# The first chunk of a fused attention and two-layer MoE kernel: its order from a list of tasks in place of a running budget

## The chip, the cores and the metric

One Trainium2 chip, one core. The metric is the device time of one execution in microseconds (us), the median of the runs shown. A core has five engines, each with its own instruction stream that it works off in order: TensorE (PE; its weight loads are listed apart as PEld), VectorE (DVE), ScalarE (ACT), GpSimd (POOL) and SyncE (SP, which here issues nearly all DMAs). An instruction that reads what another engine writes waits on a semaphore, and all that stands behind it on its engine waits too.

## The reference

```python
kv  = einsum('bhsd,bhse->bhde', k, v)            # 8 batches, 8 heads, 576 tokens, 64 wide
out = einsum('bhsd,bhde->bhse', q, kv)
out = out / sqrt(mean(out**2, -1) + 1e-6) * g_norm
x   = out, heads joined: 4608 tokens x 512
h   = max(max(x @ w1, x @ w2), x @ w3)           # layer 1, 512 -> 768
x   = h @ w_out                                  # layer 2, 768 -> 512
logits = x @ w_gate + log1p(exp(x @ w_noise)) * noise
# each token to its two best of 8 experts:  out += weight * (relu(x @ e_w1) @ e_w2)
```

All operands are float32. A product runs as three passes over values split into a high and a low part: high x high, high x low, low x high.

## The kernel before

The tokens go through in 9 chunks of 512, each as four tiles of 128. A chunk has these stages: attention (`ao`) and its norm (`norm_a` to `norm_c`); the transposes to `xT` (`xtrans_pe`, then the high part by ACT, the low part by DVE); layer 1 as 18 groups g of 12 matmuls (three passes of four, `g1_mm`), where three groups share one output block f of `h` and DVE takes their maximum (`g1_top`, split by `hsplit`); layer 2 (`g2`), 36 matmuls a tile; routing (`route_a`, `route_b`) and the scatter of rows by POOL (`scatter`). Then 25 units of expert work follow, with the weights streamed in.

The first chunk (chunk 0) is also where the layer weights come in. Weight slot s (0 to 8 for layer 1, two groups each; 9 to 11 for layer 2) arrives packed by `load_w1(s)` in one of three staging buffers and is converted in steps over ACT and DVE: `conv_lo` and `conv_sq` (ACT), `conv_hi` (two DVE instructions), `conv_add` (DVE), `conv_top` (DVE, then the high part W by ACT, line 467), `conv_rest` (DVE, the low part, line 473). The first two passes of a group read the high part of W alone, the third reads the low part. For slots 9 to 11, `gate_a` transposes the converted weight on PE and `gate_b` multiplies it by the router weights, so that layer 2 gives the logits as 16 more columns.

To have more for PE to do beside the conversion, half of chunk 1 (256 of its 512 tokens) gets its attention and its layer 1 in chunk 0 as well (`ao_early`, `xt_early`, `g1_early`: 18 groups with 256 columns); chunk 1 then does the other 256.

What sets the order: all instructions are emitted in the order of the Python program. In chunk 0 `layer1_first` decides, with a running account `T` of two times (PE and DVE) that the program adds fixed amounts to. A group is emitted whole, all three passes; `need_w` emits the rest of the slot's conversion ahead of it, and `took` emits conversion steps while the account of DVE is behind that of PE. Accumulators come from two rings of four banks, `hbank` and `abank`, each taken in turn.

Of the kernel before, what the change touches and what calls it, by code (L numbers as in the profile page):

```python
# [31 lines left out]
CST = {}  # L32
# [52 lines left out]
def body(tc, A, dbg=None):  # L85
# [205 lines left out]
    def hTf(f):  # L291
        return hTa[:, f] if f < 4 else hTb[:, f - 4]
# [4 lines left out]
    def g1_mm(g, bank, n, x=xT, t0=0, t1=512):  # L297
        s = slice((g % 2) * 128, (g % 2) * 128 + 128)
        a, b = ((0, 0), (0, 1), (1, 0))[n]
        for k in range(4):  # L300
            PE.matmul(bank[:, 0:t1 - t0], w_in(g)[:, a, k, s], x[b][:, k, t0:t1],  # L301
                      start=n == 0 and k == 0, stop=n == 2 and k == 3)

    def hsplit(f, hm, t0=0, t1=512):
        h = hTf(f)[:, :, t0:t1]
        ACT.activation(h[:, 0], hm, AF.Copy)  # L306
        DVE.tensor_tensor(h[:, 1], hm, h[:, 0].bitcast(F), op=OP.subtract)

    def g1_top(g, bank, hm):
        if g % 3 == 0:  # L310
# [13 lines left out]

    def early(f):
        return XN[f // 2][:, (f % 2) * 256:(f % 2) * 256 + 256]

    def g1_early(g):
        need_w(g // 2)
        bank = hbank()  # L330
        for z in range(3):
            g1_mm(g, bank, z, xA, 0, 256)
        took(1.42, (0.0, 0.38, 0.38)[g % 3])
        g1_top(g, bank[:, 0:256], early(g // 3))

    rows = RA.rearrange("p (i w) -> p i w", i=4)
    x2b = {}
# [125 lines left out]
    def conv_top(s):  # L463
        sq, f = w_raw(s)
        DVE.scalar_tensor_tensor(wsrc(s), sq, 2.0 ** -30, f, op0=OP.is_ge, op1=OP.mult)
        hi, lo, t = wdst(s)
        ACT.activation(hi, t, AF.Copy)  # L467
        if s + 3 < 12:
            load_w1(s + 3)

    def conv_rest(s):
        hi, lo, t = wdst(s)
# [37 lines left out]
    SP.dma_start(pad[0:64, 0:512], A["kvr"][1][:, 512:1024])  # L510
    kvraw[1] = [quarters(KV0), quarters(STG[2]), (HM[0], pad[:, 0:512])]
    load_w1(1)
    for p in range(4):
# [19 lines left out]
    for i in range(4):  # L533
        ao(0, i, abank())
        norm_a(0, i)
    conv_lo(0)
    norm_b1(0, 0, 4)
    conv_hi(0)
    conv_sq(0)
    norm_b2(0, 0, 4)  # L540
    SP.dma_start(wgn, A["wgn"])
    kvbank, tr = HB[3], []
    for i in range(4):
        norm_c(0, i)
        tr.append(xtrans_pe(0, i, None if i < 3 else abank()))
        xtrans_hi(i, tr[i])
        kv_pair(1, i, kvbank)
    hbank()
    load_q(1)
    load_w1(2)  # L550
    SP.dma_start(pad[:, 0:128], A["cst"][:, CST["tri"][0]:])
    conv_add(0)
    conv_top(0)
    conv_lo(1)
    conv_hi(1)
    conv_sq(1)
    kv_out(1, kvbank)
    for i in range(4):
        xtrans_lo(i, tr[i])
    conv_rest(0)  # L560
    conv_add(1)

    T = {"pe": 26.5, "dve": 31.0}
    steps = []
    for k in range(1, 12):
        if k < 11:
            steps.append((1.92, lambda s: (conv_lo(s), conv_hi(s), conv_sq(s)), k + 1, 0))
        steps.append((1.21, conv_top, k, 1))  # L570
# [3 lines left out]
    ready = {0: 0.0}
    whole = {0}
    gates = {"a": 0, "b": 0}
    ring = [abank]

    def step1():
        cost, fn, k, done = steps.pop(0)  # L580
        if done and k == 11 and gates["a"] == 0:
            do_gate("a")
        fn(k)
        T["dve"] += cost
        if done:
            ready[k] = T["dve"] + 1.1
        if fn is conv_rest:
            whole.add(k)

    def do_gate(x):  # L590
        (gate_a if x == "a" else gate_b)(gates[x], ring[0])
        gates[x] += 1
        T["pe"] += 0.9

    def took(pe, dve):
        T["pe"] += pe
        while steps and T["dve"] + steps[0][0] <= T["pe"]:
            step1()
        if dve:
            T["dve"] = max(T["dve"], T["pe"]) + dve  # L600

    def need_w(k):
        while k not in whole:
            step1()

    def gates_upto(j):
        while gates["b"] <= j:
            need_w(9 + gates["b"])
            if gates["a"] == gates["b"]:
                do_gate("a")  # L610
            do_gate("b")

    def g1_first(g):
        hm = X2f if g // 3 == 4 else HM[0]
        need_w(g // 2)
        if g == 0:
            first = abank(), abank()
            for z in range(3):
                for x in range(2):
                    g1_mm(x, first[x], z)  # L620
            g1_first.banks = list(first)
        bank = g1_first.banks.pop(0) if g < 2 else hbank()
        if g > 1:
            for z in range(3):
                g1_mm(g, bank, z)
        took(2.72, (0.0, 0.69, 0.69)[g % 3])
        g1_top(g, bank, hm)
        if g % 3 == 2 and g < 12:
            hsplit(g // 3, hm)
            T["dve"] += 0.79  # L630

    def ao_early():
        for i in range(2):
            ao(1, i, abank())
            norm_a(1, i, (XN[2], X2f)[i])
        norm_b1(1, 0, 2)
        norm_b2(1, 0, 2)
        for i in range(2):
            norm_c(1, i)
        took(1.9, 3.5)  # L640

    def xt_early():
        for i in range(2):
            t = xtrans_pe(1, i)
            xtrans_hi(i, t, xA)
            xtrans_lo(i, t, xA)
        took(0.9, 1.4)
        ready["x"] = T["dve"]

    def layer1_first():  # L650
        g = e = 0
        inf = 1e9
        while g < 18 or e < 18:
            rg = ready.get(g // 2, inf) if g < 18 else inf
            re = max(ready.get(e // 2, inf), ready.get("x", inf)) if e < 18 else inf
            now = T["pe"]
            if gates["a"] < 3 and ready.get(9 + gates["a"], inf) <= now and gates["a"] == gates["b"]:
                do_gate("a")
                continue
            if rg <= now or (rg < inf and rg <= re and not steps):  # L660
                T["pe"] = max(now, rg)
                g1_first(g)
                g += 1
                if g == 2:
                    ao_early()
                if g == 4:
                    xt_early()
            elif re <= now or (re < inf and not steps):
                T["pe"] = max(now, re)
                g1_early(e)  # L670
                e += 1
            else:
                nxt = min(rg, re)
                if nxt < inf and (not steps or T["dve"] >= nxt):
                    T["pe"] = nxt
                else:
                    step1()
            if gates["b"] < gates["a"]:
                do_gate("b")
        for f in (4, 5):  # L680
            hsplit(f, X2f if f == 4 else HM[0])


    order, spare = unit_order()
# [93 lines left out]
    def misc1(c, g):  # L778
# [14 lines left out]
        if c > 0:  # L793
            if g == 1:
                route_a(c - 1)
            if g == 4:
# [25 lines left out]
    def window(c):  # L822
        nx = c + 1 < NCH

        def fill(i):
            if nx and i < 2:
                ao(c + 1, i + 2, hbank())
                norm(c + 1, i + 2)

        def trans(i):  # L830
            xtrans(c + 1, i) if nx else utrans(0, i)

        if c == 0:
            ring[0] = hbank
            for j in range(3):
                gates_upto(j)
                for i in range(2):
                    g2(0, i, 2 * j, 2 * j + 2)
                if j == 1:
                    while steps:  # L840
                        step1()
                if j > 0:
                    ao(1, j + 1, hbank())
                    norm(1, j + 1, RB[:, j * 512 - 512:j * 512])
# [370 lines left out]
```

## Time and profile before

| what | value |
|---|---|
| median of 3 runs | 1627.76 us (1627.45 to 1629.03) |
| the profiled execution, its own time | 1627.63 us |
| its span in the trace | 1625.9 us |
| mean granted TensorE clock | 0.988 |
| PE busy | 1577.4 us (97%) |
| DVE busy | 743.5 us (46%) |
| ACT busy | 608.4 us (37%) |
| PE busy tenths, the first five of 40 slices | 6, 7, 9, 8, 9 (from the fifth on 9, the last 7) |

The spans of the trace begin with the first instruction. Chunk 0's layer 1 begins at 30.36 us, chunk 1's at 170.23, chunk 2's at 228.26. A row of a timeline gives the start, the duration, the engine, the line and operation, output<-input, and in brackets the engine's idle time ahead of it and who ended that. Equal instructions that follow one another are one row with a count.

### The profile page before, as it was taken

Reading aid. Unit: us, or ns where it says so; the run is one execution under the profiler, and the core shown is the slowest. Engines: PE = TensorE matmul, PEld = TensorE weight load, DVE = VectorE, ACT = ScalarE, POOL = GpSimd, SP = SyncE. Lnnn points to the kernel's source line nnn. Section 1 sums busy time; section 2 is a strip of 40 time slices with the busy share of each in tenths; the row PEclk is TensorE's granted clock in tenths of the full one; section 3 lists DMA queues with packets and bytes.
Section 4 is the critical chain, followed back from the end, with each engine's and each line's share of the span. In section 5 each row is a group of like instructions: output and inputs, shape, how many; then the busy total and the mean of one; then the engine's idle time right before and its main releaser. Section 6 shows DMA issues by size and latency. Waiting matters only on the chain.

```text
span 1625.9 us, 21935 instructions
## 1 busy us (share of the span) xinstructions
PE 1577.4 (97%) x8716; PEld 1370.7 (84%) x8716; DVE 743.5 (46%) x1416; ACT 608.4 (37%) x981; POOL 225.9 (14%) x326
## 2 busy tenths in 40 slices
PE   6798999999999999999999999999999999999997
PEld 6678998988889898989788888888888888888886
DVE  5675443434333343454544355364354444534443
ACT  3443331313232222323233355454354443544433
POOL 0000201111020202021311121111021010210102
PEclk9898999999999999999999999999999999999998
DMA  7220481202030301051554476575474564746543
GB/s 280 97 89 23 175 313 52 105 33 112 26 137 15 123 27 53 1 182 56 197 170 138 125 222 181 182 209 166 156 220 132 179 169 143 206 135 204 146 146 73
DMA packets 52572, 219.43 MB, mean 135 GB/s; under 512 B 6896, under 2 KB 7152, under 8 KB 34928
## 3 DMA queue, kind: packets, MB, share of 16 engines
q1 hardware_dynamic: 32608, 166.50, 28.6%
q0 software_dynamic: 19856, 51.48, 13.6%
q8 instruction: 70, 1.15, 0.3%
q14 instruction: 38, 0.31, 0.1%
HBM read 166.49 MB, written 51.47 MB: 134 GB/s over the span
## 4 chain that ended last, share of the span: by engine, by line
PE 93%; DVE 3%; ACT 1%; DMA 0%; issue 0%; POOL 0%; SPq 0%; DVEq 0%; POOLq 0%; ACTq 0%
PE bank L301 26%; PE bank L1086 24%; PE bank L1024 24%; PE bank L348 10%; PE bank L743 2%; PE bank L188 2%; PE bank L209 2%; PE bank L1038 1%; PE bank L263 1%; DMA G<-mw 0%; PE bank L488 0%; DVE G L452 0%; DVE W L473 0%; DVE G L895 0%; PE bank L212 0%
## 5 line engine op out<-in xcount | busy, mean ns | idle before, releaser
L301 PE MATMUL bank<-B,W 128*128 128x512 f32 (+1 forms) x2160 | 459.9, 373 | 16.9 <-ACT W L467 11.4
L301 PEld LDWEIGHTS bank<-B,W 128*128 128x128 f32 x2160 | 377.6, 191 | 87.2 <-ACT W L467 12.6
L1086 PE MATMUL bank<-W,B 128*128 128x512 f32 x1728 | 421.1, 390 | 0.9 <-ACT hm L1091 0.9
L1086 PEld LDWEIGHTS bank<-W,B 128*128 128x128 f32 x1728 | 320.0, 188 | 64.8 <-ACT hm L1091 1.4
L1024 PE MATMUL bank<-B,W 128*128 128x512 f32 (+1 forms) x1728 | 356.9, 344 | 0.4 <-issue 0.4
L1024 PEld LDWEIGHTS bank<-B,W 128*128 128x128 f32 x1728 | 278.0, 189 | 40.7 <-issue 0.6
L283 DVE TENSOR_TENSOR W<-G,W 128x1024 fp32r<-128x1024 f32 x200 | 242.6, 1225 | 131.6 <-ACT W L282 131.3
L1028 ACT ACTIVATE B<-bank 128x512 fp32r<-128x512 f32 (+1 forms) x176 | 91.5, 520 | 372.0 <-PE bank L1024 354.9
L1029 DVE SCALAR_TENSOR_TENSOR B<-bank,B 128x512 fp32r<-128x512 f32 (+1 forms) x176 | 104.4, 594 | 270.8 <-ACT B L1028 269.0
L282 ACT ACTIVATE W<-G 128x1024 fp32r<-128x1024 f32 x200 | 207.8, 1055 | 47.3 <-PE bank L1086 39.3
L348 PE MATMUL bank<-W,B 128*128 128x256 f32 (+1 forms) x1296 | 172.3, 291 | 0.1
L348 PEld LDWEIGHTS bank<-W,B 128*128 128x128 f32 x1296 | 164.1, 192 | 1.6 <-ACT W L492 0.7
L414 POOL DMA_INDIRECT Xg<-RA,si x72 | 74.5, 1035 | 539.6 <-ACT hm L311 372.2
L313 DVE TENSOR_TENSOR hm<-hm,bank 128x512 f32<-128x512 f32 (+1 forms) x106 | 69.5, 656 | 132.1 <-PE bank L301 128.7
L306 ACT ACTIVATE B<-hm 128x512 fp32r<-128x512 f32 (+1 forms) x53 | 32.2, 607 | 195.2 <-DVE hm L313 174.8
L1024 PE MATMUL bank<-xlo,W 128*128 128x512 f32 x384 | 102.8, 389 | 0.0
L1060 POOL DMA_INDIRECT out<-xn,idt x37 | 62.1, 1677 | 280.9 <-ACT xn L1091 273.7
L1024 PEld LDWEIGHTS bank<-xlo,W 128*128 128x128 f32 x384 | 72.1, 188 | 15.3
L1060 POOL DMA_INDIRECT out<-x2T,idt x19 | 30.9, 1629 | 272.8 <-ACT x2T L1091 270.4
L747 ACT ACTIVATE B<-bank 128x512 fp32r<-128x512 f32 x76 | 41.7, 596 | 45.0 <-PE bank L743 42.3
L311 ACT ACTIVATE hm<-bank 128x512 f32<-128x512 f32 (+1 forms) x53 | 30.5, 576 | 65.9 <-PE bank L301 54.7
L353 ACT ACTIVATE RA<-bank 128x256 f32<-128x256 f32 x72 | 26.1, 386 | 76.0 <-PE bank L348 76.0
(191 smaller groups left out, 1046.1 us busy)
## 6 DMA issues: line engine op xcount, KB each, us to landing
G<-mw SPq DMA_DIRECT2D x100, 1024.0 KB, 4.9
RB<-Xg SPq DMA_DIRECT2D x13, 1028.0 KB, 7.2
G<-w1s SPq DMA_DIRECT2D x12, 1024.0 KB, 5.0
out<-pad POOLq DMA_DIRECT2D x1, 9472.0 KB
kv<-kv SPq DMA_DIRECT2D x8, 1024.0 KB
G<-kv SPq DMA_DIRECT2D x8, 1024.0 KB, 17.1
RB<-qT SPq DMA_DIRECT2D x8, 1024.0 KB, 5.5
RA<-Xg SPq DMA_DIRECT2D x8, 514.0 KB
```

Of the source, the lines that this page charges most:

```text
L282: ACT.activation(w[:, 0:1024], src, AF.Copy)
L283: DVE.tensor_tensor(w[:, 1024:2048], src, w[:, 0:1024].bitcast(F), op=OP.subtract)
L301: PE.matmul(bank[:, 0:t1 - t0], w_in(g)[:, a, k, s], x[b][:, k, t0:t1], start=n == 0 and k == 0, stop=n == 2 and k == 3)
L313: DVE.tensor_tensor(hm, hm, bank, op=OP.max)
L348: PE.matmul(x2b[i][z][:, 0:hi - lo], h[:, a, s], w[:, b, lo:hi], start=f == 0 and n == 0, stop=f == 5 and n == 2)
L414: i = POOL.indirect_dma_start(out=Xg, out_offset=bass.IndirectOffsetOnAxis(ap=idx, axis=0), in_=src, in_offset=None)
L747: ACT.activation(x[0][:, :, s], t, AF.Copy)
L1024: PE.matmul(bank[:, 0:n], w[:, a, k, s], x[b][:, k, 0:n], start=z == 0, stop=z == 11)
L1028: ACT.activation(h[:, 0, 0:n], bank[:, 0:n], AF.Relu)
L1029: DVE.scalar_tensor_tensor(h[:, 1, 0:n], bank[:, 0:n], 0.0, h[:, 0, 0:n].bitcast(F), op0=OP.max, op1=OP.subtract)
L1060: d = POOL.indirect_dma_start(out=A["out"], out_offset=bass.IndirectOffsetOnAxis(ap=idt[u % 3][:, i:i + 1], axis=0), in_=y, in_offset=None ...
L1086: PE.matmul(obank[i], h[:, a, s], w[:, b, ff % 2, :], start=ff == 0 and n == 0, stop=ff == 7 and n == 2)
```

## The change

`layer1_first` with its account `T`, and the code ahead of it from the first conversion on, give way to a list of tasks. Each has a name, an engine, a length, the names of the tasks that it needs, and an urgency; `run_tasks` takes, step after step, the task that can begin first by these lengths (ties within 0.04 go to the lower urgency number) and emits it. Several functions are cut in two for it (`norm_a`, `hsplit`, `conv_top`), and a group of layer 1 becomes two tasks: passes 0 and 1 (`gp`), which need the high part of W, and pass 2 (`gq`), which needs the low part. The matrix work and the conversions are the same instructions in another order. All gates are now emitted ahead of layer 2; `out` emits layer 2 for tiles 0 and 1 behind them. In chunk 1, `route_b` and the first scatter go from group 4 to group 7, the second scatter from group 8 to group 12. `load_w1(s + 3)` still follows the step that frees its buffer.

```diff
-    T = {"pe": 26.5, "dve": 31.0}
...
-    def took(pe, dve):
-        T["pe"] += pe
-        while steps and T["dve"] + steps[0][0] <= T["pe"]:
-            step1()
...
+    def run_tasks(free):
+        end = {}
+        while tasks:
+            best = None
+            for x in tasks:
+                name, eng, cost, after, fn, urgency, hb = x
+                need = list(after)
+                if hb:
+                    taken = ring_users + [hb] * hb[1]
+                    need += [u[0] for u in taken[:-4]]
+                if any(n not in end for n in need):
+                    continue
+                at = max([free[eng]] + [end[n][0] + 0.1 * (end[n][1] != eng) for n in need])
+                key = (at, urgency)
+                if best is None or at < best[0][0] - 0.04 or (at < best[0][0] + 0.04 and urgency < best[0][1]):
+                    best = (key, x)
...
+            fn()
+            end[name] = at + cost + (2.0 if eng == "SP" else 0.0), eng
+            free[eng] = at + cost
...
+        u = 2 + 0.1 * s
+        task(f"lo{s}", "ACT", 1.15, [f"w{s}"], lambda s=s: conv_lo(s), u)
+        task(f"op{s}", "DVE", 1.92, [f"w{s}"] + free_t, lambda s=s: conv_hi(s), u)
...
+        task(f"rest{s}", "DVE", 1.22, [f"hi{s}"], lambda s=s: conv_rest(s), u - 1)
...
+            task(f"gp{g}", "PE", 1.82, ["x0l3", f"hi{g // 2}", "first2"] + ([f"gq{g - 1}"] if g > 2 else []),
+                 lambda g=g: passes(g, [0, 1]), 2, on_ring(f"ev{g}"))
+            task(f"gq{g}", "PE", 0.91, [f"gp{g}", f"rest{g // 2}"], lambda g=g: passes(g, [2]), 1)
...
+    for e in range(18):
+        task(f"eq{e}", "PE", 1.44, ["x1l0", "x1l1", f"rest{e // 2}"] + ([f"eq{e - 1}"] if e else []),
+             lambda e=e: early_passes(e), 3, on_ring(f"ee{e}"))
...
-            if g == 4:
+            if g == (7 if c == 1 else 4):
                 route_b(c - 1)
                 scatter(c - 1, 0)
-            if g == 8:
+            if g == (12 if c == 1 else 8):
                 scatter(c - 1, 1)
...
-            layer1_first()
+            run_tasks({"PE": 16.1, "DVE": 17.4, "ACT": 16.8, "SP": 14.0})
```

Three places of the built order follow. In the names, `W_70` to `W_78` are slots 0 to 8, `G_82` to `G_84` the staging buffers, `B_85` the transposed tokens of chunk 0 and `B_87` those of half of chunk 1, `bank_105` to `bank_108` the ring of `hbank`. The lines of the changed file stand a few lines lower (301 is 308 there, 467 is 474).

ACT around the high part of slot 0 (`W_70`), before:

```order
L267 ACTIVATE B_85<-bank_109,gn 128x4x128
L467 ACTIVATE W_70<-RA 128x1024
L439 ACTIVATE G_83<-G_83 128x1024
L448 ACTIVATE G_83<-G_83 128x1024
L198 COPY kvbd_91<-bank_108 64x4x64
L311 ACTIVATE hm_96<-bank_110 128x512
```

and now:

```order
L274 ACTIVATE B_85<-bank_109,gn 128x4x128
L444 ACTIVATE G_83<-G_83 128x1024
L198 COPY kvbd_91<-bank_108 64x4x64
L474 ACTIVATE W_70<-RA 128x1024
L453 ACTIVATE G_83<-G_83 128x1024
L229 ACTIVATE xn_95<-bank_112 128x512
```

The copy of the second batch's products (`kvbd_91`) and one step of slot 1 now stand ahead of slot 0's high part.

PE in slots 1 to 3 of layer 1, before (12 matmuls are a whole group):

```order
L301 MATMUL bank_105<-B_85,W_71 128x512 x12
L301 MATMUL bank_106<-B_85,W_71 128x512 x12
L263 MATMUL bank_107<-cst,xn_95 128x128 x4
L263 MATMUL bank_108<-cst,x2T_97 128x128 x4
L301 MATMUL bank_105<-B_87,W_70 128x256 x12
L301 MATMUL bank_106<-B_87,W_70 128x256 x12
L301 MATMUL bank_107<-B_85,W_72 128x512 x12
L301 MATMUL bank_108<-B_85,W_72 128x512 x12
```

and now:

```order
L308 MATMUL bank_105<-B_85,W_71 128x512 x12
L308 MATMUL bank_106<-B_85,W_71 128x512 x8
L270 MATMUL bank_107<-cst,xn_95 128x128 x4
L270 MATMUL bank_108<-cst,x2T_97 128x128 x4
L308 MATMUL bank_106<-B_85,W_71 128x512 x4
L308 MATMUL bank_105<-B_87,W_70 128x256 x12
L308 MATMUL bank_106<-B_87,W_70 128x256 x12
L308 MATMUL bank_107<-B_85,W_72 128x512 x8
L308 MATMUL bank_108<-B_87,W_71 128x256 x12
L308 MATMUL bank_107<-B_85,W_72 128x512 x4
L308 MATMUL bank_105<-B_85,W_72 128x512 x12
L308 MATMUL bank_106<-B_85,W_73 128x512 x8
```

From slot 2 on, a group of 256 columns stands between the passes on the high part (x8) and the pass on the low part (x4).

PE at the first gate, before (`wgn` are the router weights, `W_79` is slot 9, in layer 2):

```order
L301 MATMUL bank_108<-B_87,W_78 128x256 x12
L480 MATMUL bank_105<-cst,RA 128x128 x4
L480 MATMUL bank_106<-cst,RA 128x128 x4
L488 MATMUL bank_107<-wgn,G_82 128x16 x8
L348 MATMUL bank_110<-W_79,B_86 128x256
```

and now:

```order
L308 MATMUL bank_108<-B_85,W_78 128x512 x12
L485 MATMUL bank_105<-cst,RA 128x128 x4
L485 MATMUL bank_106<-cst,RA 128x128 x4
L308 MATMUL bank_107<-B_87,W_75 128x256 x12
L308 MATMUL bank_108<-B_87,W_75 128x256 x12
L493 MATMUL bank_105<-wgn,G_82 128x16 x8
L308 MATMUL bank_106<-B_87,W_76 128x256 x12
L485 MATMUL bank_107<-cst,RA 128x128 x4
L485 MATMUL bank_108<-cst,RA 128x128 x4
```

Eight groups of 256 columns are kept back for the three gates and stand between their steps.

## Rows read from the trace of the kernel before

**Rows 1.** Waits of weight loads, 30.3 to 229 us: total, how often, longest

```profile
PEld bank L301 <- ACT W L467: 12.6, 6, 8.5
PEld bank L301 <- DVE W L473: 4.7, 5, 1.4
PEld bank L488 <- ACT G L481: 3.2, 3, 1.9
PEld bank L480 <- DVE RA L465: 3.1, 1, 3.1
PEld L400 <- issue: 2.0, 1, 2.0
PEld bank L301 <- DVE B L272: 1.3, 2, 0.9
PEld bank L301 <- DVE hm L313: 1.2, 1, 1.2
PEld bank L301 <- ACT B L267: 1.2, 1, 1.2
```

**Rows 2.** Stretches: busy us by engine (instructions), then PEclk, DMA share, GB/s

```profile
43.20:53.40 10.20, 6.08 (x14) 4.84 (x15) 5.84 (x6) 2.19 (x2) 0.00 (x0) 0.50 0.31 104
53.50:135.30 81.80, 71.93 (x415) 61.29 (x414) 58.87 (x71) 35.73 (x45) 0.00 (x0) 1.00 0.25 91
135.40:142.20 6.80, 6.80 (x31) 6.62 (x31) 4.05 (x6) 3.09 (x4) 0.00 (x0) 0.50 0.00 0
155.80:159.20 3.40, 3.40 (x18) 3.40 (x17) 0.17 (x1) 0.77 (x2) 1.28 (x5) 0.51 0.03 5
179.70:183.10 3.40, 3.40 (x18) 3.40 (x17) 2.33 (x10) 1.72 (x5) 0.00 (x0) 0.50 0.02 8
```

**Rows 3.** Timeline where layer 1 of chunk 0 begins

```profile
29.37 0.39 PE L188 MATMUL bank<-pad,hm 128*128 128x128 f32 x2
29.86 0.42 DVE L198 COPY kvbd<-bank 64x256 f32<-64x256 f32 x1 [3.04 <-PE bank L188]
30.36 2.11 PE L301 MATMUL bank<-B,W 128*128 128x512 f32 x8 [0.60 <-ACT W L467]
...
37.88 1.16 PE L209 MATMUL bank<-kvbd,kv 128*128 128x128 f32 x8
38.00 0.60 ACT L225 ACTIVATE xn<-bank 128x512 f32<-128x512 f32 x1 [1.34 <-PE bank L212]
```

**Rows 4.** Timeline of PE in chunks 1 and 2, groups back to back

```profile
193.86 6.00 PE L301 MATMUL bank<-B,W 128*128 128x256 f32 x48
...
228.26 11.06 PE L301 MATMUL bank<-B,W 128*128 128x512 f32 x48
```

**Rows 5.** Timeline of DVE, back to back, and of ACT beside it

```profile
72.31 1.06 ACT L467 ACTIVATE W<-RA 128x1024 fp32r<-128x1024 f32 x1 [0.51 <-DVE RA L465]
73.33 0.41 DVE L313 TENSOR_TENSOR xn<-xn,bank 128x256 f32<-128x256 f32 x1
...
73.66 1.22 DVE L473 TENSOR_TENSOR W<-RA,W 128x1024 fp32r<-128x1024 f32 x1
74.80 0.69 DVE L443 TENSOR_SCALAR RB<-G 128x1024 int32<-128x1024 int32 x1
75.52 1.23 DVE L444 SCALAR_TENSOR_TENSOR RB<-G,RB 128x1024 int32<-128x1024 int32 x1
...
76.66 1.22 DVE L465 SCALAR_TENSOR_TENSOR RA<-G 128x1024 f32<-128x1024 f32 x1
```

**Rows 6.** Waits of DVE, 30 to 160 us: total, how often, longest

```profile
DVE hm L313 <- PE bank L301: 11.7, 9, 4.3
```

**Rows 7.** The page's DMA issues: size, median us to landing

```profile
G<-w1s SPq DMA_DIRECT2D x12, 1024.0 KB, 5.0
```

**Rows 8.** Timeline of chunk 1: its first groups, and where DVE comes back

```profile
170.23 5.92 PE L301 MATMUL bank<-B,W 128*128 128x256 f32 x48
...
178.79 0.41 DVE L313 TENSOR_TENSOR hm<-hm,bank 128x256 f32<-128x256 f32 x1
```

More of the change, by code (lines that the diff above doesn't have):

```diff
@@ L574, in body @@
[L574 to L593, printed above, removed]
@@ L595, in took @@
-    def took(pe, dve):
-        T["pe"] += pe
-        while steps and T["dve"] + steps[0][0] <= T["pe"]:
-            step1()
[L599 to L622, printed above, removed]
-        if g > 1:
[L624 to L630, printed above, removed]
@@ L632, in ao_early @@
-    def ao_early():
-        for i in range(2):
[L634 to L665, printed above, removed]
-                if g == 4:
[L667 to L681, printed above, removed]
@@ new lines, in passes, with hm0 @@
+    def passes(g, z):
+        if g not in bank_of:
+            bank_of[g] = abank() if g < 2 else hbank()
+        for n in z:
+            g1_mm(g, bank_of[g], n)
+    def hm0(g):
+        return X2f if g // 3 == 4 else HM[0]
+    for z in range(3):
+        task(f"first{z}", "PE", 1.82, [["x0h3", "hi0", "n0c2"], ["x0l3", "first0"], ["rest0", "first1"]][z],
+             lambda z=z: (passes(0, [z]), passes(1, [z])), 2)
+    for g in range(18):
+        if g > 1:
+            task(f"gp{g}", "PE", 1.82, ["x0l3", f"hi{g // 2}", "first2"] + ([f"gq{g - 1}"] if g > 2 else []),
+                 lambda g=g: passes(g, [0, 1]), 2, on_ring(f"ev{g}"))
+            task(f"gq{g}", "PE", 0.91, [f"gp{g}", f"rest{g // 2}"], lambda g=g: passes(g, [2]), 1)
+        f = g // 3
+        hm_free = [f"split{f - 1}"] if g % 3 == 0 and 0 < f < 4 else ["x1t1"] if g == 12 else []
+        hm_free = ["split3"] if g == 15 else hm_free
+        task(f"ev{g}", "DVE" if g % 3 else "ACT", 0.69 if g % 3 else 0.58,
+             [f"gq{g}" if g > 1 else "first2", "kvp3"] + ([f"ev{g - 1}"] if g else []) + hm_free,
+             lambda g=g: g1_top(g, bank_of[g], hm0(g)), 0.5)
@@ new lines, in body @@
+    last = [f"eq{e}" for e in range(18)]
+    for f in range(6):
+        task(f"hi_h{f}", "ACT", 0.61, [f"ev{3 * f + 2}"] + (last if f > 3 else []), lambda f=f: hsplit_hi(f, hm0(3 * f)), 0.5)
+        task(f"split{f}", "DVE", 0.72, [f"hi_h{f}"], lambda f=f: hsplit_lo(f, hm0(3 * f)), 0.5)
+    x1 = {0: XN[2], 1: X2f}
+    for i in range(2):
+        task(f"ao{i}", "PE", 0.92, ["q1", "kvo", "x0l3"] + (["ao0"] if i else []), lambda i=i: ao(1, i, abank()), 0)
+        task(f"n1s{i}", "ACT", 0.6, [f"ao{i}", f"t0{i + 2}"], lambda i=i: norm_sq(1, i, x1[i]), 0.5)
+        task(f"n1r{i}", "DVE", 0.69, [f"n1s{i}"], lambda i=i: norm_red(1, i), 0.5)
@@ new lines, in early_passes @@
+    def early_passes(e):
+        bank_of["e", e] = hbank()
+        for z in range(3):
+            g1_mm(e, bank_of["e", e], z, xA, 0, 256)
+    for e in range(18):
+        task(f"eq{e}", "PE", 1.44, ["x1l0", "x1l1", f"rest{e // 2}"] + ([f"eq{e - 1}"] if e else []),
+             lambda e=e: early_passes(e), 3, on_ring(f"ee{e}"))
+        task(f"ee{e}", "DVE" if e % 3 else "ACT", 0.42 if e % 3 else 0.36,
+             [f"eq{e}", "x1t0", "x0h3"] + ([f"ee{e - 1}"] if e % 3 else []),
+             lambda e=e: g1_top(e, bank_of["e", e][:, 0:256], early(e // 3)), 0.5)
@@ new lines, in body @@
+    for j in range(3):
+        task(f"gate_a{j}", "PE", 0.9, [f"top{9 + j}"] + ([f"gate_b{j - 1}"] if j else []),
+             lambda j=j: gate_a(j, hbank), 1.5, on_ring(f"gate_a{j}", 2))
+        task(f"gate_w{j}", "ACT", 1.2, [f"gate_a{j}"], lambda: None, 0)
+        task(f"gate_b{j}", "PE", 0.9, [f"gate_w{j}", f"rest{9 + j}"], lambda j=j: gate_b(j, hbank), 1.5,
+             on_ring(f"gate_b{j}"))
+        for i in range(2):
+            task(f"out{i}{j}", "PE", 1.5,
+                 [f"gate_b{j}", f"split{2 * j + 1}", "gq17"] + (["rest11", "gate_a2"] if j == 2 else [])
+                 + ([f"out{i}{j - 1}"] if j else []),
+                 lambda i=i, j=j: g2(0, i, 2 * j, 2 * j + 2), 4 + 0.1 * j + 0.01 * i)
@@ L684, in body @@
+    for i in (2, 3):
+        task(f"ao{i}", "PE", 0.92, ["rest11", f"ao{i - 1}"], lambda i=i: (ao(1, i, hbank()), norm(1, i, RB[:, i * 512 - 1024:i * 512 - 512])),
+             3.5, on_ring(f"ao{i}"))
     order, spare = unit_order()
```

127 lines of the change are left out of this document (70 added, 57 removed).

## The prediction

> **What bounds the kernel now.** I read the page first: PE is busy nearly everywhere except in the first slices, so only the first chunks can give anything large; behind them each chunk is a solid run of matmuls, and a change that ends chunk 1 earlier ends the kernel earlier by as much. Next came the waits of the weight loads from layer 1 of chunk 0 to the start of chunk 2 [rows 1]. I take the weight loads since a matmul's modelled end covers part of a wait, while a late weight load shows all of it. The reader should see two kinds there. Nearly all of it is PE waiting for the weight conversion: for the high part (12.6 us, 8.5 of it at slot 1), for the low part (4.7) and for the gates (3.2 and 3.1). In chunk 1 there are two for the routing, on line 400 (2.0) and on a maximum behind it (1.2). The rows add up to 29.3; 0.6 to 0.8 of that lies ahead of 30.36, where layer 1 begins, so 28.5 are left.
>
> Third, the granted clock [rows 2]. Four stretches ran at half the full clock (0.50, that is 1.2 GHz), and each came behind PE idling or doing little. PE was busy in them for 6.08, 6.80, 3.40 and 3.40 us; what is done at half the clock takes twice as long, so half of 19.68, or 9.8 us, was lost. Waits and clock together: 38.3 us between 30.36 and 228.26 that are no work. This is the ceiling of a better order.
>
> **What is moved, part by part.** The instructions are the same in number and kind; nothing is added or removed but semaphore waits. So the sum is what goes of the 38.3, less what is late in the new order.
>
> *The start.* ACT's high part of slot 0 now stands behind the copy of the second batch's products, which needs PE's last product (29.37 + 0.39 = 29.76). DVE copies its half (to 30.28), ACT its half (I take DVE's 0.42; to 30.75), then the high part takes 1.06 [rows 3, 5]; with three handovers of about 0.1 the first matmul is at 32.1 instead of 30.36: 1.8 us lost. Its bounds are 1.5 (no handovers) and 2.5.
>
> *Slot 1, which waited 8.5 us.* Before, its conversion stood behind the first maximum and the whole norm of chunk 1. Now DVE's order from 30.3 is: first step of slot 1 (0.72 + 1.14), low part of slot 0, add, top (1.14 each), which ends at 35.6. These spacings are between starts in [rows 5]: 0.33 for a 256-wide maximum, 1.14 for a 1024-wide operation of 1.22, 0.72 for line 443, so that a 512-wide operation of about 0.69 costs about 0.61. Then DVE waits for the square of the first attention tile: PE does two passes over two groups (16 matmuls of 11.06 / 48 = 0.230, 3.7 us [rows 4]) and the tile (about 1.1 [rows 3]), until 36.9, ACT squares (0.60 [rows 3]), 37.6. Two reductions, slot 2's first step, a maximum, small ones and the low part of slot 1 come to 5.1: 42.7. PE, which now does both high passes first, gets to that low part at 32.1 + 3.7 + 2 x 1.1 + 16 x 0.230 = 41.7 without counting anything else. So 8.5 becomes 1.0 to 1.6; I take 1.6.
>
> *Slots 2 to 8.* The other 4.1 us for high parts and most of the 4.7 for low parts came in pieces, at slot after slot (the longest for a low part 1.4). In the new order a 256-wide group (12 x 6.00 / 48 = 1.5 us [rows 4]) stands between the high passes and the low pass, which covers the 1.2 of the low part's subtraction. This holds while DVE is ahead. Counted in DVE's new order from the copy at 30.3 to slot 9's top, which releases the first gate: nine slots of 0.72 + 4 x 1.14 (47.5), ten 512-wide maxima, four splits, two reductions, two norms, two low parts of tokens (20 x 0.61 = 12.2), six 256-wide maxima (2.0), small ones (1.0): 62.7, so 93.0, or 95.0 with the 2.0 of waiting above. PE until that gate has 216 wide matmuls (49.7), ten 256-wide groups (15.0) and tiles and transposes (about 3): 32.1 + 67.7 + 2.1 of waits = 101.9. PE is the later one by 7 us; if its 36 operations of 1.14 took their full 1.22, by 4. Both run nearly full, which is new: the lead is small, and I charge 0.5 for late tokens at the first 256-wide group. Weight loads cost nothing: one lands 5.0 us after its issue [rows 7], and it is issued two slots (10.6 us of DVE) ahead of its use; without that cover each slot would lose up to 5.
>
> *The gates.* 6.3 us before. Each now has two 256-wide groups between its transposes and its product, and one ahead of the next gate. The next gate's top stands in DVE behind the previous gate's small evictions, so PE may catch up. Bounds per gate are 0 and 3.1, the longest before; I take 0.8, near the low end, since 4.5 us of PE work stand between: 1.8 for the two that follow a gate and some rest.
>
> *Chunk 1.* The wait on line 400 goes, because that matmul stands three groups later. What is late next is the ring of banks: the sixth group needs the bank of the second, whose maximum stands in DVE behind the routing. It ended 8.97 us after the chunk's start (178.79 + 0.41 - 170.23 [rows 8]), and PE gets there after five groups (7.5 us): 1.5 to 1.9 stays, of 3.2. The moved scatters cost nothing on POOL or in DMA: the last one is four groups (6 us) later, and the rows it reads are overwritten only after the six groups left and the first tile of layer 2; without that cover the copy of the first tile would wait.
>
> *The clock.* Two waits of about 2 us in a row at the start, the gates and the wait in chunk 1 are the places where it can still fall. Of four stretches I keep two short ones like the third and fourth of [rows 2]: 1.7 each, 3.4. Bounds are 0 and the 9.8 of before.
>
> **Sum.** Now lost: 1.8 + 1.6 + 0.5 + 1.8 + 1.9 + 3.4 = 11.0. Gain: 38.3 - 11.0 = 27.3. Against the profiled execution's own 1627.63 (its span and 1.7 around it; the median 1627.76 is 0.1 above) that gives 1600.3; I say 1600.
>
> The Trainium skill, "TensorE: Matmul & The Clock Gate", section "Back-to-back issue gap", gives 131 ns as the sustained spacing of 512-wide matmuls; the trace has 230 [rows 4]. By the page PE's 216 wide matmuls would take 28 instead of 50 us, DVE would be the later one at the first gate (95 against 80), and the sum would be 1593. The measurement decides here, so I give this no chance of its own.
>
> **The rivals.**
>
> *DVE becomes the bound.* Its evictions stand between conversions in a fixed order, and each waits if PE is not there yet. Before, nine of them waited 11.7 us, 1.3 each [rows 6]. If all 16 up to slot 9's top did, DVE would get there at 93.0 + 20.8 = 113.8, 12 after PE: 1612. Against it: PE now has groups of both kinds in stock, so that evictions are mostly due; it decides from 7 us of such waits on.
>
> *The clock stays as patchy as before.* If 9.8 instead of 3.4 are lost: 1607. For it speak the two early waits and the gates; against it that 53.50 to 135.30 ran at 1.00 [rows 2] with the waits of slots 2 to 8 in it.
>
> *The lengths of the list don't hold and nothing is gained.* The order was made for lengths that don't all fit this trace (a start with PE free at 16.1, though it finishes its tiles about then). If slots go on paying their pieces and only the 8.5 shrinks: 28.5 keeps 21, the time is about 1620. The order above speaks against it, since the covering group is there whatever the lengths.
>
> *Slower.* Finer mixing of 512-wide and 256-wide groups with short waits could hold the clock at half over the whole of layer 1 in chunk 0, from 32 to 123. About 85 us of full-clock work would then take up to 85 more. It is slower than before from 31 us of full-clock work run at half (27.3 gained and the 3.4 counted). Half of the stretch would give 1639. Rows of the second stretch [rows 2] speak against it, with a full clock at the same kind of mix.
>
> **How the numbers follow.** Forecast (1594 to 1605) 0.72; DVE bound 0.12; patchy clock 0.09; nothing much gained 0.04; slower 0.03. The low end, 1594, is the sum without any half clock (1597) and with half of the remaining waits gone as well. For eight times in ten I leave out the tail beyond 1608 (most of the DVE case above it, and the two last cases) and what falls below 1594: 1594 to 1608. A change under 0.2% (3.3 us) can't be told from none here. Faster by more: all but the last case and a part of the one before, 0.96; the same: 0.01; slower: 0.03.
>
> **What would show it.** In the changed profile: the first 512-wide group on slot 0 near 32; no wait over 2 us on line 474's high part, and few on the low part between 50 and 100; PE over 95% and DVE over 85% busy there; the first transposes of a gate near 102; chunk 1 near 143 and chunk 2 near 201, after which everything is as before, only earlier. It is wrong in its main step if PE waits for the low or high part at slot after slot, in the clock's term if stretches at 0.50 add up to more than 10 us, and in the claim that the gain is kept if chunk 2 begins early and the span is not shorter by as much.

## The result and the profile after

| | before | after |
|---|---|---|
| median (lowest to highest) | 1627.80 us of 4 runs (1627.45 to 1629.03) | 1599.48 us of 4 runs (1597.54 to 1599.92) |
| profiled execution, its own time | 1627.63 us | 1599.92 us |
| its span | 1625.9 us | 1598.1 us |
| layer 1 of chunk 0 begins | 30.36 us | 31.99 us |
| chunk 1 begins (timeline of the matmuls) | 170.23 us | 143.54 us |
| chunk 2 begins | 228.26 us | 198.90 us |

The ratio is 0.9822 (95% interval 0.9805 to 0.9839): 28.3 us between the medians and 27.7 between the profiled executions, where 27.3 were worked out and 1600 predicted. The page shows where, in its busy times and in PE's busy tenths over 40 slices: of the first four slices, which read 6, 7, 9 and 8 before, the second and the fourth are now 9.

```profile
PE 1567.1 (98%) x8716; PEld 1364.4 (85%) x8716; DVE 742.3 (46%) x1416; ACT 608.4 (38%) x981; POOL 224.7 (14%) x326
PE   6999999999999999999999999999999999999997
```

The waits of the weight loads from layer 1 of chunk 0 to chunk 2 (total, how often, longest) answer to [rows 1]:

```profile
PEld bank L308 <- ACT W L474: 2.2, 1, 2.2
PEld bank L308 <- DVE hm L326: 1.9, 1, 1.9
PEld bank L308 <- DVE W L478: 1.5, 1, 1.5
PEld bank L485 <- DVE RA L470: 1.3, 2, 0.7
PEld bank L308 <- ACT B L274: 0.4, 1, 0.4
PEld bank L212 <- issue: 0.4, 1, 0.4
PEld bank L308 <- DVE B L279: 0.3, 1, 0.3
PEld bank L209 <- issue: 0.2, 1, 0.2
```

The wait for the high part was 12.6 us in six pieces; one is left, at the start. The low part went from 4.7 in five to 1.5 in one, the gates from 6.3 to 1.3, chunk 1 from 3.2 to 1.9. Stretches of the same trace (busy us by engine, then granted clock, DMA share, GB/s) answer to [rows 2]:

```profile
32.72:36.13 3.41, 3.41 (x10) 2.65 (x9) 3.11 (x3) 0.82 (x1) 0.00 (x0) 0.50 1.01 428
50.00:100.00 50.00, 49.89 (x274) 43.57 (x275) 47.48 (x55) 28.47 (x33) 0.00 (x0) 1.00 0.42 148
752.93:756.34 3.41, 3.41 (x13) 2.95 (x13) 3.17 (x10) 1.79 (x3) 0.00 (x0) 0.50 0.00 0
200.00:700.00 500.00, 500.00 (x2883) 439.03 (x2883) 195.93 (x572) 135.87 (x273) 62.59 (x112) 1.00 0.22 82
```

From 50 to 100 us PE is 99.8% busy and DVE 95%, all at the full clock. The only half-clock stretch between layer 1's start and chunk 2 is the first row. The third row is new: it lies far behind, in the expert part. The timeline gives the places that the prediction worked out one by one (start, duration, engine, and in brackets the idle time ahead and who ended it); it answers to [rows 3] and [rows 8] (the last row before a jump can stop where the stretch that was asked for stops, and its count with it):

```profile
30.05 0.42 DVE L198 COPY kvbd<-bank 64x256 f32<-64x256 f32 x1 [0.81 <-PE bank L188]
...
30.50 0.37 ACT L198 COPY kvbd<-bank 64x256 f32<-64x256 f32 x1 [2.13 <-DVE kvbd L198]
30.88 1.06 ACT L474 ACTIVATE W<-RA 128x1024 fp32r<-128x1024 f32 x1
31.99 1.19 PEld L308 LDWEIGHTS bank<-B,W 128*128 128x128 f32 x5 [2.23 <-ACT W L474]
...
38.59 0.60 ACT L229 ACTIVATE xn<-bank 128x512 f32<-128x512 f32 x1 [5.06 <-PE bank L212]
...
43.12 1.22 DVE L478 TENSOR_TENSOR W<-RA,W 128x1024 fp32r<-128x1024 f32 x1
44.39 0.77 PEld L308 LDWEIGHTS bank<-B,W 128*128 128x128 f32 x4 [1.51 <-DVE W L478]
...
98.42 1.22 DVE L470 SCALAR_TENSOR_TENSOR RA<-G 128x1024 f32<-128x1024 f32 x1
102.16 1.02 PEld L485 LDWEIGHTS bank<-cst,RA 128*128 128x128 f32 x8
...
152.56 2.94 PEld L308 LDWEIGHTS bank<-B,W 128*128 128x128 f32 x24 [1.86 <-DVE hm L326]
```

The chain at the start is there as described: DVE's copy, ACT's copy, the high part of slot 0, and then PE. The first gate's transposes begin at 102.16 (102 was expected), 2.5 us after the slot's top ended at 99.64. The waits of DVE from 30 to 160 us show that its evictions into `hm` are now nearly always due, against 11.7 us in [rows 6]. With those into `xn` and `x2T`, which [rows 6] does not list, 20.7 us became 3.0. What it waits for at the start is the square of the first attention tile:

```profile
DVE stat L233 <- ACT xn L229: 3.3, 1, 3.3
DVE hm L326 <- PE bank L308: 1.7, 5, 0.6
```

### The profile page after: what moved, and what is told of

The parts are those of the page before. It is cut to its first block, busy times and chain, and to the rows that moved or that the text cites. A ratio compares the mean times of both kernels' runs of the same rounds, so it can differ in the third digit from the quotient of the medians.

```text
span 1598.1 us, 21920 instructions
## 1 busy us (share of the span) xinstructions
PE 1567.1 (98%) x8716; PEld 1364.4 (85%) x8716; DVE 742.3 (46%) x1416; ACT 608.4 (38%) x981; POOL 224.7 (14%) x326
## 4 chain that ended last, share of the span: by engine, by line
PE 96%; DVE 1%; DMA 1%; ACT 1%; issue 0%; POOL 0%; SPq 0%; POOLq 0%; DVEq 0%
PE bank L308 27%; PE bank L1092 25%; PE bank L1030 25%; PE bank L353 10%; PE bank L760 2%; PE bank L188 2%; PE bank L209 2%; PE bank L1044 1%; PE bank L270 1%; DMA RB<-qT 1%; DMA G<-mw 0%; PE bank L493 0%; PE bank L212 0%; POOL out L1066 0%; PE bank L485 0%
## 5 line engine op out<-in xcount | busy, mean ns | idle before, releaser
L353 PE MATMUL bank<-W,B 128*128 128x256 f32 (+1 forms) x1296 | 167.5, 287 | 0.0
L1066 POOL DMA_INDIRECT out<-hm,idt x19 | 33.0, 1736 | 143.6 <-ACT hm L1097 139.9
```

The source lines that it names most:

```text
L353: PE.matmul(x2b[i][z][:, 0:hi - lo], h[:, a, s], w[:, b, lo:hi], start=f == 0 and n == 0, stop=f == 5 and n == 2)
L1066: d = POOL.indirect_dma_start(out=A["out"], out_offset=bass.IndirectOffsetOnAxis(ap=idt[u % 3][:, i:i + 1], axis=0), in_=y, in_offset=None ...
```

## The experiments

All ratios are to the kernel before, run beside each; `gates_last`, `dve_load`, `dve_load2` and `start` ran on another chip than the other experiments. Chunk 2 is where its first 512-wide group starts in the profiled run. The last column is the span from there on.

| run | median us (runs) | ratio, 95% interval | chunk 2 | behind it |
|---|---|---|---|---|
| before | 1627.80 (4) | 1 | 228.26 | 1397.6 |
| after | 1599.48 (4) | 0.9822 (0.9805 to 0.9839) | 198.90 | 1399.2 |
| slot1_first | 1626.86 (8) | 0.9994 (0.9983 to 1.0006) | 229.18 | 1397.1 |
| route_only | 1626.14 (10) | 0.9993 (0.9984 to 1.0003) | 225.33 | 1399.1 |
| lengths_one | 1612.55 (2) | 0.9901 (0.9872 to 0.9930) | 212.96 | 1399.1 |
| whole_groups | 1599.29 (2) | 0.9820 (0.9791 to 0.9848) | 199.01 | 1398.7 |
| gates_last | 1598.04 (2) | 0.9814 (0.9784 to 0.9844) | 199.89 | 1397.2 |
| route_back | 1602.05 (2) | 0.9837 (0.9808 to 0.9865) | 202.28 | 1397.3 |
| dve_load | 1598.18 (2) | 0.9815 (0.9786 to 0.9843) | 198.69 | 1397.2 |
| dve_load2 | 1602.05 (2) | 0.9839 (0.9810 to 0.9867) | 202.21 | 1398.6 |
| start | 1594.83 (2) | 0.9794 (0.9766 to 0.9823) | 195.79 | 1397.2 |
| route_spread | 1598.37 (2) | 0.9822 (0.9804 to 0.9840) | 197.83 | 1399.3 |
| all | 1594.46 (5) | 0.9792 (0.9779 to 0.9806) | 194.38 | 1398.7 |

The last column moves by 2.2 us between kernels whose order there is the same, so chunk 2 is the sharper measure of an edit ahead of it.

**Can the kernel before simply be mended at slot 1?** Its norm and transposes of chunk 1 are emitted one group later, behind slot 1's conversion.

```diff
-                if g == 2:
+                if g == 3:
                     ao_early()
-                if g == 4:
+                if g == 5:
                     xt_early()
```

> The kernel before with one part of the new order alone: the attention tiles and the norm of half of chunk 1 come one group later (behind group 2 instead of 1), so that slot 1's conversion no longer stands behind them. Theory (the gain comes from the order as a whole; a stall taken out at one place comes back at others as long as groups are emitted whole and the conversion waits behind other work): the 8.5 us wait at slot 1 shrinks to about 5, new waits of 3 to 6 appear at slots 2 and 3, and chunk 2 begins at 221 to 226 instead of 228.3; the time falls by 2 to 6 us. Rival (one misplaced norm is the main fault): the wait goes and nothing takes its place, the half-clock stretch behind it goes too, chunk 2 begins near 217 and the time falls by about 11.

Measured: nothing gained. The 8.5 us at slot 1 became 5.3, and the waits for the high part went from 12.6 in all to 19.6; its weight loads:

```profile
41.93 4.77 PEld L301 LDWEIGHTS bank<-B,W 128*128 128x128 f32 x12 [5.34 <-ACT W L467]
57.64 3.93 PEld L301 LDWEIGHTS bank<-B,W 128*128 128x128 f32 x12 [5.94 <-ACT W L467]
76.98 10.19 PEld L301 LDWEIGHTS bank<-B,W 128*128 128x128 f32 x44 [2.94 <-ACT W L467]
```

The wait at slot 1 did shrink as expected once the norm no longer stood ahead of the conversion, but the gain was not there: with the fixed account the same work is late at the next slots. The big wait was a symptom of the whole order, not a fault at one place.

**What are the lengths worth?** All tasks get the same length, the dependences and urgencies stay.

```diff
-        tasks.append((name, eng, cost, after, fn, urgency, hb))
+        tasks.append((name, eng, 1.0, after, fn, urgency, hb))
```

> The changed kernel, with every task's length in the list set to 1.0; dependences and urgencies stay. Theory (the lengths make the order, since they say which engine is free first): PE waits come back, about 10 us more of them than in the changed kernel, chunk 2 begins at 207 to 212 instead of 198.8 and the time is 8 to 14 us above it. Rival (dependences and the cut of groups in two do it, lengths are a detail): chunk 2 begins within 2 us of 198.8.

Measured: chunk 2 14.1 us later than in the changed kernel, 15.3 us earlier than before. The 15.3 hold the later routing in chunk 1 as well, which this run keeps (2.9 by `route_only` below). So some 12 us come with the list, its dependences and urgencies, and 14 with the lengths. Its waits of weight loads:

```profile
PEld bank L485 <- DVE RA L470: 3.3, 2, 2.1
PEld bank L353 <- ACT RA L358: 2.9, 2, 1.4
PEld bank L308 <- ACT W L474: 2.9, 3, 1.8
PEld bank L308 <- DVE W L478: 1.9, 1, 1.9
```

They came back in small pieces at the gates, in layer 2 and at the slots, together with 10.2 us at half the clock (129.3 to 136.1 and 146.4 to 149.8).

**Does the 256-wide group between the passes cover the low part?** The two tasks of a 512-wide group are made one again, which in the list needs both parts.

```diff
-            task(f"gp{g}", "PE", 1.82, ["x0l3", f"hi{g // 2}", "first2"] + ([f"gq{g - 1}"] if g > 2 else []),
-                 lambda g=g: passes(g, [0, 1]), 2, on_ring(f"ev{g}"))
-            task(f"gq{g}", "PE", 0.91, [f"gp{g}", f"rest{g // 2}"], lambda g=g: passes(g, [2]), 1)
+            task(f"gq{g}", "PE", 2.73, ["x0l3", f"rest{g // 2}", "first2"] + ([f"gq{g - 1}"] if g > 2 else []),
+                 lambda g=g: passes(g, [0, 1, 2]), 2, on_ring(f"ev{g}"))
```

> The changed kernel, with each 512-wide group again one task of three passes that needs the low part of its slot. What the prediction said (a 256-wide group between the passes covers the subtraction): without it the low parts are waited for again, 0.5 to 1 us at each of seven slots, chunk 2 begins at 202 to 206. Rival (the list makes up for it by putting 256-wide groups ahead of the whole group, as DVE is ahead anyway): chunk 2 begins within 1 us of 198.8 and the cut in two was not needed.

Measured: no difference (199.01 against 198.90). Its only wait for a low part (slot 1, as in the changed kernel), the subtraction of slot 4's low part, and PE's matmuls between 67.4 and 68.5 us (shape, count, busy us):

```profile
PEld bank L308 <- DVE W L478: 1.5, 1, 1.5
...
67.31 1.22 DVE L478 TENSOR_TENSOR W<-RA,W 128x1024 fp32r<-128x1024 f32 x1
...
L308 PE MATMUL bank<-B,W 128*128 128x256 f32 x11 | 1.5, 282 | 0.0
```

No wait for a low part has appeared from slot 2 on, though nothing stands between the passes. But the edit moves the 256-wide groups and does not take them away: as the rival said, the list now puts one to three of them ahead of each slot's 512-wide groups, and slot 4's subtraction runs beside one. A part that ends later than that still has the group's own two high passes: slot 3's ended at 62.20, in a group that began at 61.76. So the place between the passes is not needed, and the cut of the groups in two gains nothing that shows here. Whether slots 2 to 8 would go without any 256-wide group in stock was not tried; in the changed kernel the group between the passes is used, by little (slot 5's low part ended at 75.63, 0.5 us after that group began).

**Do the 256-wide groups between the gates' steps cover those?** All gates wait until both kinds of groups are through.

```diff
-        task(f"gate_a{j}", "PE", 0.9, [f"top{9 + j}"] + ([f"gate_b{j - 1}"] if j else []),
+        task(f"gate_a{j}", "PE", 0.9, [f"top{9 + j}", "gq17", "eq17"] + ([f"gate_b{j - 1}"] if j else []),
```

> The changed kernel, with each gate made to wait for all groups of layer 1, so that no 256-wide group is left to stand between a gate's steps. What the prediction said (those groups cover the gates): waits at the gates go from 1.3 back towards the 6.3 of the kernel before, chunk 2 begins at 202 to 204. Rival (what cost time before was that slot 9 to 11 were converted late on DVE, not where the gate stood; the conversion is early now): waits at the gates stay at or below 1.5 and chunk 2 begins at 197 to 199.5.

Measured: the gates wait no more than with groups between them (1.0 against 1.3):

```profile
PEld bank L353 <- DVE W L498: 0.5, 1, 0.5
PEld bank L493 <- ACT G L486: 0.5, 1, 0.5
```

Chunk 2 is 1.0 later, but in this run 152.27 to 155.68 was at half the clock, which costs 1.7 by itself. So the groups need not stand between a gate's steps. Here too they are moved and not taken away: all eight now run ahead of the first gate (the first row counts the matmuls between 102.3 and 113.3 us), and meanwhile DVE does the top of slot 10, the second gate's:

```profile
L308 PE MATMUL bank<-B,W 128*128 128x256 f32 x94 | 11.4, 283 | 0.0
...
105.77 1.22 DVE L470 SCALAR_TENSOR_TENSOR RA<-G 128x1024 f32<-128x1024 f32 x1
```

In the changed kernel that top is not done early. It stands in DVE behind an eviction of the gate before, as the prediction said, and the second and third gate wait 0.66 us each for theirs:

```profile
108.26 0.19 DVE L498 TENSOR_TENSOR W<-bank,W 128x32 fp32r<-128x32 f32 x1 [2.38 <-ACT W L497]
...
108.70 1.22 DVE L470 SCALAR_TENSOR_TENSOR RA<-G 128x1024 f32<-128x1024 f32 x1
```

**How far is DVE ahead?** One reduction of 400 columns with an unused result is added to each slot's conversion (ten by 106 us; in `dve_load2` two a slot, 18 ahead of the first gate). Two of them take 1.08 us of DVE (55.83 to 56.91), so about 5 and 9.7 us are added.

```diff
+        for _ in range(DVE_MORE):
+            DVE.tensor_reduce(tmp[:, 0, :], cst[:, 0:400].rearrange("p (a b) -> p a b", a=8), axis=AX.X, op=OP.add)
```

> The changed kernel, with one more DVE reduction (400 elements, about 0.5 us) in each slot's conversion, of which the list knows nothing: 4.5 us more on DVE until slot 9's top, 6 us in all. It computes nothing that is used. Theory as predicted (DVE leads PE by 4 to 7 us at the first gate): hidden, chunk 2 begins within 1 us of 198.8. Rival, from the trace of the changed kernel (slot 9's top ended at 99.64, its use on PE began at 102.16, so DVE leads by 2.5): at least 2 us show, chunk 2 begins at 200.5 to 203.

> The same with two such reductions in each slot, 9 us until slot 9's top and 12 us in all. If DVE leads by 4 to 7 us: 2 to 5 us show (chunk 2 at 201 to 204). If it leads by 2.5: about 6.5 us show (chunk 2 at 204.5 to 207). If DVE had been the bound all along, all of it would show (chunk 2 at 208 to 211). In each case new waits on the low part of slots 2 to 8 are where it shows.

Measured: the first 5 us are hidden (198.69). With 9.7, chunk 2 is 3.3 later, and high parts (not the low parts that were expected) are late at slot after slot; the weight loads of `dve_load2`:

```profile
67.74 6.78 PEld L309 LDWEIGHTS bank<-B,W 128*128 128x128 f32 x36 [1.31 <-ACT W L477]
75.03 15.25 PEld L309 LDWEIGHTS bank<-B,W 128*128 128x128 f32 x84 [0.50 <-ACT W L477]
91.38 6.78 PEld L309 LDWEIGHTS bank<-B,W 128*128 128x128 f32 x36 [1.10 <-ACT W L477]
98.66 6.77 PEld L309 LDWEIGHTS bank<-B,W 128*128 128x128 f32 x36 [0.51 <-ACT W L477]
```

Counted from the start of layer 1, which was at 31.4 in both runs and at 31.99 in the changed kernel, 0.4 and 3.9 us show. About 5 to 6 us are to spare. In the changed kernel's rows 2.5 of that is the lead at the first gate, and 2.5 is DVE's idle time between 50 and 100 (50.00 - 47.48). So "the lead is small" holds: DVE is the next bound, some 5 us away.

**The routing in chunk 1.** In `route_back` the changed kernel has it at the old groups; in `route_only` the kernel before has it at the new ones.

```diff
-            if g == (7 if c == 1 else 4):
+            if g == 4:
...
-            if g == (12 if c == 1 else 8):
+            if g == 8:
```

> The changed kernel, with the routing and the scatters of chunk 1 back at groups 4 and 8. Theory: PE waits twice again in chunk 1 (about 2 on the routing's matmul and 1.2 on the maximum) instead of once 1.9, so chunk 2 begins 1.1 to 1.5 us later, and up to 1.7 more if the clock falls behind it as it did in the kernel before. Rival: the waits overlap and the move was worth nothing (under 0.3).

> The kernel before with nothing but the later routing in chunk 1 (route_b and the first scatter at group 7, the second at group 12). Theory: the wait of 2.0 us on the routing goes, the one behind the maxima stays at 1.5 to 1.9 of 3.2 in all, so 1.3 to 1.7 us; the half-clock stretch of chunk 1 (1.7) may go with it. Chunk 2 begins at 225.3 to 227.0 instead of 228.26, time 1624.5 to 1626.5. Rival (the move is worth nothing in the old order, since the same maxima are late behind the routing anyway): chunk 2 at 228.3, time 1627.8.

Measured: `route_back` is 3.4 us later at chunk 2. Both old waits are back, and behind them 151.24 to 158.07 ran at half the clock with PE busy for 5.88 of it, 2.9 lost:

```profile
150.85 0.10 PEld L405 LDWEIGHTS <-onesb 128*128 128x128 bf16 x1 [1.96 <-issue]
...
152.19 9.93 PEld L308 LDWEIGHTS bank<-B,W 128*128 128x128 f32 x61 [1.21 <-DVE hm L326]
```

(2.0 + 1.2 - 1.9 is 1.3 of waits; the clock's 2.9 explains the rest with some to spare. The same two waits had only 3.41 us at half the clock behind them in the kernel before [rows 2], so the 3.4 is not the price of the old routing alone.) `route_only` ends chunk 1 earlier by 2.9 us, 1.3 of it in waits (1.87 instead of 3.2) and the 1.7 of the half-clock stretch at 179.7 in [rows 2], which is gone. Its time is only 1.3 us shorter and not told from none by the interval: behind chunk 2 its profiled run was 1.5 longer, with a half-clock stretch of 3.41 at 779.7 that before has not.

**What is left of the waits: the start.** ACT's half of the copy of the second batch's products becomes a task of its own behind slot 0's high part.

```diff
-    task("kvo", "DVE", 0.42, ["kvp3"], lambda: kv_out(1, bank_of["kv"]), 0)
+    task("kvo", "DVE", 0.42, ["kvp3"], lambda: kv_half(1, bank_of["kv"], 0), 0)
+    task("kvp", "ACT", 0.37, ["kvo", "hi0"], lambda: kv_half(1, bank_of["kv"], 1), 0)
```

> The changed kernel, with ACT's half of the copy of the second batch's products as a task of its own behind slot 0's high part. Theory (the 2.2 us wait at the start is the one place that the new order made worse, since the copy stood ahead of slot 0): the first matmul on slot 0 begins near 30.5 instead of 32.0, the half-clock stretch that followed at 32.7 goes too, chunk 2 begins 1 to 3 us earlier (196 to 198). Rival (slot 1 is the limit a little later anyway, it waited 1.5 us for its low part): PE begins earlier and waits longer there, and chunk 2 begins at 198 to 199.

Measured: layer 1 begins 1.65 us earlier, and the half-clock stretch behind its wait is gone; chunk 2 is 3.1 earlier (1.65 and 1.7 add up to 3.35).

```profile
29.23 1.06 ACT L477 ACTIVATE W<-RA 128x1024 fp32r<-128x1024 f32 x1 [0.89 <-DVE RA L473]
30.34 2.84 PEld L311 LDWEIGHTS bank<-B,W 128*128 128x128 f32 x13 [0.63 <-ACT W L477]
```

**What is left: chunk 1, and all together.** `route_spread` cuts the first part of the routing in four, at groups 2 to 5 instead of all at group 1, with what follows one group later. `all` has that, the edit of `start`, and 256-wide groups taken ahead where a 512-wide one could begin at the same time.

```diff
-            if g == 1:
+            if c > 1 and g == 1:
                 route_a(c - 1)
-            if g == (7 if c == 1 else 4):
+            if c == 1 and g in (2, 3, 4, 5):
+                route_part(0, (2, 3, 4, 5).index(g))
+            if g == (8 if c == 1 else 4):
...
-             lambda e=e: early_passes(e), 3, on_ring(f"ee{e}"))
+             lambda e=e: early_passes(e), 0.9, on_ring(f"ee{e}"))
```

> The changed kernel with the first part of the routing of chunk 0 cut in four, at groups 2, 3, 4 and 5 of chunk 1 instead of all at group 1, and the rest one group later. Theory (the 1.9 us that stayed in chunk 1 are maxima behind the routing on DVE): the wait falls to 0.5 to 0.9, chunk 2 begins at 197.5 to 198.0 instead of 198.90, time 1598.0 to 1598.5 where the expert part is as in the changed kernel, 1596.5 to 1597 without its half-clock stretch. Rival (the bank ring itself is short, whatever DVE does between): the wait stays at 1.9, chunk 2 at 198.9.

> The changed kernel with three edits: ACT's half of the copy of the second batch's products behind slot 0's high part (as in start), the routing spread over groups 2 to 5 of chunk 1 (as in route_spread), and groups of 256 columns taken ahead of the passes of a 512-wide group where both can begin (urgency 0.9 instead of 3). Theory (what is left at the start and in chunk 1 adds up, 3.1 + 1.2): chunk 2 begins at 194 to 195, time 1592.5 to 1594.5, ratio to before 0.9785 to 0.9795. Rival (what is gained at one place is waited for at the next, DVE being nearly full): chunk 2 at 196 or later, time 1595 to 1599.

Measured: in `route_spread` the wait that stayed is halved, and chunk 2 is 1.1 earlier:

```profile
156.06 2.94 PEld L308 LDWEIGHTS bank<-B,W 128*128 128x128 f32 x24 [0.95 <-DVE hm L326]
```

So at least half of the 1.9 us was the maxima behind the routing on DVE, and not the ring of banks by itself; what holds the other 0.95 was not tried. `all` begins chunk 2 at 194.38, 4.5 us earlier than the changed kernel and as expected; its three longest waits:

```profile
PEld bank L311 <- DVE W L490: 1.7, 1, 1.7
PEld bank L311 <- DVE hm L329: 1.4, 2, 0.9
PEld bank L311 <- ACT B L277: 0.7, 1, 0.7
```

It is faster than the changed kernel (1592.02 to 1595.47 against 1597.54 to 1599.92), but its 1.4 us over `start` at chunk 2 don't show in the medians (1594.46 and 1594.83, on different chips).

## Why the prediction was right, and where its reasons were not

**The sum.** Of the 38.3 us that were no work before, by the rows above these are left ahead of chunk 2:

| term | predicted | measured |
|---|---|---|
| start of layer 1 | 1.8 | 1.6 (31.99 - 30.36) |
| slot 1's low part | 1.6 | 1.5 |
| late tokens | 0.5 | 0.7 (0.4 + 0.3) |
| gates | 1.8 | 1.3 |
| chunk 1 | 1.9 | 1.9 |
| half clock | 3.4 | 1.7 (one stretch of 3.41) |
| sum | 11.0 | 8.7 |

38.3 - 8.7 is 29.6, and chunk 2 did begin 29.4 us earlier. The term that was mis-sized is the clock's: two stretches were kept, and the gates and chunk 1 gave none. The start's own terms (29.76, two copies of 0.42, 1.06 and three handovers of 0.1) add up to 31.96 and not to 32.1; 31.99 was measured. By its sign for the start ("no wait over 2 us on line 474's high part") the prediction contradicted this sum: the 1.8 that it added to the 0.6 of before make 2.4, and 2.2 was measured. The weight loads took longer to land than was put (a median of 8.4 us on the page of the changed kernel, not 5.0), and still no wait of PE's weight loads is for one of them.

**The lead of DVE.** The prediction had DVE through slot 9's top at 95.0 and PE at the first gate at 101.9, a lead of 7 us, or 4. Measured were 99.64 and 102.16, a lead of 2.5. DVE's work was counted rightly (62.7 against the 63.27 busy us below), its waits were not: 6.0 us in place of 2.0, the row's length less its busy time.

```profile
30.39:99.65 69.26, 66.43 (x356) 56.30 (x357) 63.27 (x76) 40.28 (x49) 0.00 (x0) 0.98 0.45 168
```

The longest is the 3.3 for the square of the first attention tile. The half-clock stretch stood in the matmuls ahead of that tile: the first 16 of layer 1 took 5.53 us and the next 16 3.91. So the term of the clock, put down for PE alone, cost DVE as well.

**Given back later.** The claim that behind chunk 2 all stays as before is off by 1.6 us, and this is why 27.7 and not 29.4 arrive at the end. The weight loads there:

```profile
748.08 2.00 PEld L1092 LDWEIGHTS bank<-W,B 128*128 128x128 f32 x9
751.34 0.19 PEld L1092 LDWEIGHTS bank<-W,B 128*128 128x128 f32 x1 [1.26 <-issue]
752.05 0.19 PEld L1092 LDWEIGHTS bank<-W,B 128*128 128x128 f32 x1 [0.53 <-issue]
752.77 0.19 PEld L1092 LDWEIGHTS bank<-W,B 128*128 128x128 f32 x1 [0.53 <-issue]
```

In the first expert unit PE stood three times for 2.3 us in all, for nothing that the profile shows, and the clock fell for 3.41 us behind it: 1.7 lost. All waits of the weight loads behind chunk 2 add up to 6.9 us against 7.0 before, so the clock is the difference. The prediction came out nearer than its terms because these 1.6 and the 2.3 too much in its sum have opposite signs.

**The covering groups.** The step on slots 2 to 8 (a 256-wide group "stands between the high passes and the low pass, which covers the 1.2 of the low part's subtraction") and the one on the gates ("4.5 us of PE work stand between") were right in their cost. Their cause is not shown as it was put: `whole_groups` and `gates_last` move these groups to another place, and nothing returns, so the place between is not what the gain rests on. That a stock of them is needed somewhere is neither shown nor refuted, since no run took them away. What the runs do show is that DVE's order carries the gain: its evictions into `hm` are due when their turn comes (11.7 us of waits became 1.7), lengths that say nothing cost 14.1 us, and some 5 us of added work on DVE stay hidden.

**The rivals.** DVE as the bound is refuted with the unchanged work, and `dve_load2` shows its start: from some 5 to 6 us of added work on, where 7 us of waits were put. The patchy clock did not come, with 1.7 us lost instead of 9.8. "The lengths of the list don't hold and nothing is gained" (1620) was too dark: with lengths that say nothing at all the time is 1612.55. The slow clock over the whole mix is refuted by 1.00 from 50 to 100.

The Trainium skill's 131 ns for a 512-wide matmul ("TensorE: Matmul & The Clock Gate", "Back-to-back issue gap"), by which DVE would have been the later engine, is not borne out: 48 of them took 11.06 us in chunk 2 of `start` as in [rows 4], 230 ns each, and PE was the later one at the first gate.

## What to carry to other kernels

A large wait on one conversion is not mended by moving the step ahead of it: with two nearly full engines the order of both has to be made together, from what each step needs and how long it takes, and the lengths are worth at least as much as the dependences. Look for what is left where the new order begins and ends, at the first instruction that it put behind another (3.1 us here) and at the stage that it hands over to (1.1 us). And when a cover is named, take it away in an experiment, and look in the trace where it went: here two edits that should have taken covers away only moved them ahead.

## What was not expected of the hardware

The part behind chunk 2 was between 1397.1 and 1399.3 us long for the same work. The waits of the weight loads from 205 to 1600 us, their rows added up, are 6.6 us in `start` (1397.2 behind chunk 2), 6.5 in `gates_last` (1397.2), 9.0 in `route_spread` (1399.3), and 6.9 with 1.7 of half clock in the changed kernel (1399.2). The difference is in the first expert units: gaps of up to 1.3 us that the profile calls issue, or a wait of 1.0 to 2.1 for DVE, in one run at one line and in the next at another. What makes them was not tried, and stays open; they are about as large as what `route_spread` gained.

A wait costs more than its own time where the clock falls behind it. The 1.9 us wait in chunk 1 of the changed kernel had the full clock behind it; in `gates_last` the same wait took 2.2 and had 3.41 us at 0.50 behind it; in `route_back` 2.0 and 1.2 in a row had 6.83, where the same two had 3.41 in the kernel before [rows 2] and in `slot1_first` (from 180.02). Edits of one microsecond in this place thus moved chunk 2 by 1.1 to 3.4.
